# Moving the last token search behind five pairs of outputs, with MoE products over four PSUM banks, in a fused cross-covariance attention and mixture-of-depths kernel

## The chip, the cores and the metric

The kernel runs on one core of a Trainium2 chip. The metric is the time on the device in microseconds. Its engines are TensorE (PE in the profile; PEld is its weight load), VectorE (DVE), ScalarE (ACT), GpSimd (POOL) and SyncE (SP). SP only issues DMAs here; POOL issues DMAs too, the loads and the indirect ones.

## The reference

Two stages, over 4 batches of 6208 rows and 256 channels.

```python
qn = q / (norm(q, axis=1) + 1e-6);  kn = k / (norm(k, axis=1) + 1e-6)
a = softmax(kn.transpose(0, 2, 1) @ qn / tau)          # 256 x 256 per batch
x = v @ a                                              # 6208 x 256 per batch
scores = x @ w_gate                                    # one per row
for each batch: top = the 128 rows of the largest scores
    ye = relu(x[top] @ w1) @ w2                        # 256 -> 1024 -> 256
    out[top] = x[top] + sigmoid(scores[top]) * ye      # all other rows: out = x
```

Attention runs over channels, so all rows of q and k have to be read before the first row of the output can be computed. The 128 rows with the largest scores are known only when all scores of the batch are.

## The kernel before, in words

**Tiling.** A batch is cut into six chunks of 1024 rows (128 partitions of 8 rows) and a remainder of 64 rows. All loads of q, k and v are issued by POOL (`emit_load`, L166) and cast to bf16 on the way. The outputs of a chunk are collected in a tile `stage` of 1 MB and stored by one DMA of SP's queue (`emit_store`, L534).

**The main part.** For each batch a first pass accumulates the product of q and k (`s_ps`, L291) and the squares (`g_ps`, L293, L295) in PSUM. The softmax (`softmax_stages`) follows in small steps. The second pass transposes v (L403), evicts it (L410, L412), multiplies by the softmax matrix to give the output rows (`o_ps`, L477) and by the gate weights to give the scores (`sc_ps`, L431). An output pair is four matmuls (two rows of each partition) in one PSUM bank, evicted by one copy (L483 on VectorE or L485 on ScalarE). The order of all this is a written list, `plan` (L125 to L148). Batch 0 and 1 have their second pass inside the first pass of the following batch. Of batch 2 (`E`) most outputs, and of batch 3 (`L`) all of them, are left for the end; two late groups of batch 1 (`H`) get their MoE rows added by matmuls in `late_pair`.

**The search.** `select_stages` (L548) is a generator that finds the 128 rows with the largest scores: the scores are scaled to a range in which the threshold lies (`u`, L577), then seven rounds count the rows over seven thresholds (L585 or L587 compare, L591 counts on VectorE, a matmul at L598 sums over the partitions, L601 picks the interval). Then come the row numbers (L608 to L637) and an indirect DMA that gathers the rows of v (L641). `mlp_stages` (L649) is the MoE of one batch in steps: two transposes (L654), the attention product (L660), two transposes (L669), the gate (L674 to L679), the first product and Relu (L687, L690), the second product (L695), the update (L704) and an indirect DMA that scatters the rows into the output (L710). The scatter of a batch has to wait for the stores of that batch.

**The tail.** When all scores of batch 3 are there, the code from L838 on runs: two steps of the last search (its scores and maximum, then the scaling and the first comparison), the deferred stores, and then a loop of 40 output pairs: 15 of batch 2, then 25 of batch 3. After each pair `between` (L450) may take one more step of the last search, or, when that is at its end, one step of the MoE of batch 2:

```python
            due = pairs[0] in (2, 4, 6) or pairs[0] > 6 and pairs[0] % 5 in (0, 3)
            if due and not advance(side):
                advance_all(side2)
```

So the step that begins with the matmul of the first count (L598) is put into TensorE's order behind the second pair. All engines take their instructions in order. While the search runs, ScalarE evicts every pair; after it VectorE and ScalarE take turns (L482). In this loop `out_psum` (L438) hands out four banks in turn: one of `s_ps`, one of `g_ps` (both free by then) and the two of `ps_o`. Before the loop it hands out the two of `ps_o` alone. After the loop the store of the late chunk of batch 1 is issued, then 24 matmuls on constants (`keep_warm`, L415), the MoE of batch 3, and its scatter as the last transfer.

Of the kernel before, what the change touches and what calls it, by code (L numbers as in the profile page):

```python
# [9 lines left out]
F32 = mybir.dt.float32  # L10
# [4 lines left out]
ALU = mybir.AluOpType  # L15
AX = mybir.AxisListType

P = 128
# [1 line left out]
CHUNK = RPP * P  # L20
NTHR = 7
NSTEP = 7
NEG = -3.0e38


@with_exitstack
def kernel(
# [12 lines left out]
    nc = tc.nc  # L40

    B, N, C = q.shape
# [8 lines left out]
    REM = N - NFULL * CHUNK  # L51
    assert 0 < REM <= P
    NCOL = NFULL * RPP + 1
# [20 lines left out]
    moe = ctx.enter_context(tc.tile_pool(name="moe", bufs=1))  # L74
# [5 lines left out]
    ps_o = ctx.enter_context(tc.tile_pool(name="ps_o", bufs=2, space=PS))  # L80
# [69 lines left out]
    for op in plan:  # L150
        if op[0] in ("p1", "T"):
            u = ("qk", op[1], op[2]) if op[0] == "p1" else ("v", op[1], op[2][0])
# [102 lines left out]
    for i in range(NSTEP):  # L255
        w = 1.0 / (NTHR + 1) ** (i + 1)
        nc.vector.tensor_scalar(out=shares[:, i, :], in0=iota_row[:, 1:NTHR + 1], scalar1=w,
                                scalar2=None, op0=ALU.mult)
# [7 lines left out]
                            scalar2=None, op0=ALU.mult)  # L266
# [148 lines left out]
    def keep_warm(n):  # L415

        bank = ps_o.tile([P, 2, C], F32, name="o_ps")
        for _ in range(n):
            nc.tensor.matmul(bank[:, 0, 0:P], lhsT=ident_b, rhs=ones_b, start=True, stop=True)
# [18 lines left out]
    def out_psum():  # L438

        if now[0] <= B:  # L440
            return ps_o.tile([P, 2, C], F32, name="o_ps")
        turn[0] += 1
        if turn[0] % 4 == 1:
            return ps_s.tile([P, 2, C], F32, name="s_ps")
        if turn[0] % 4 == 3:
            return ps_g.tile([P, 4, P], F32, name="g_ps").rearrange("p a c -> p (a c)").rearrange(
                "p (a c) -> p a c", a=2)
        return ps_o.tile([P, 2, C], F32, name="o_ps")

    def between():  # L450

        if now[0] > B:
            pairs[0] += 1
            due = pairs[0] in (2, 4, 6) or pairs[0] > 6 and pairs[0] % 5 in (0, 3)
            if due and not advance(side):
                advance_all(side2)

    pairs = [0]
# [89 lines left out]
    def select_stages(b):  # L548

        sc_ps = sc_tiles[b]  # L550
        sc = moe.tile([P, NCOL], F32, name="sc")
        nc.vector.memset(sc[:, NCOL - 1:NCOL], NEG)
        u = moe.tile([P, NCOL], F32, name="u0")
        nc.vector.memset(u[:, NCOL - 1:NCOL], -1.0)  # L554
        nc.vector.tensor_reduce(out=sc[:, 0:NCOL - 1], in_=sc_ps[:, 0:NCOL - 1, :], axis=AX.X, op=ALU.add)
        nc.vector.tensor_reduce(out=sc[:REM, NCOL - 1:NCOL], in_=sc_ps[:REM, NCOL - 1:NCOL, :],
                                axis=AX.X, op=ALU.add)
# [8 lines left out]
        lo = moe.tile([P, 1], F32, name="lo")  # L566
        tops = moe.tile([P, 8], F32, name="tops")
        rng = moe.tile([P, 1], F32, name="rng")
        nc.vector.tensor_reduce(out=lo, in_=mps[:, 0:P], axis=AX.X, op=ALU.min)
        nc.vector.max(out=tops, in_=mps[:, 0:P])  # L570
        nc.vector.tensor_scalar(out=rng, in0=tops[:, 2:3], scalar1=lo, scalar2=1e-30, op0=ALU.subtract,
                                op1=ALU.max)
        nc.vector.reciprocal(rng, rng)


        for rows, cols in ((slice(0, P), slice(0, NCOL - 1)), (slice(0, REM), slice(NCOL - 1, NCOL))):
            nc.vector.tensor_scalar(out=u[rows, cols], in0=sc[rows, cols], scalar1=lo[rows], scalar2=rng[rows],  # L577
                                    op0=ALU.subtract, op1=ALU.mult)
        delta = None
        for i in range(NSTEP):  # L580
            cmp = moe.tile([P, NTHR, NCOL], BF16, name="cmp", bufs=2)
# [4 lines left out]
            else:  # L586
                nc.vector.scalar_tensor_tensor(out=cmp, in0=wide, scalar=delta, in1=thr,  # L587
                                               op0=ALU.subtract, op1=ALU.is_ge)
# [3 lines left out]
            if i > 0:  # L592
                nxt = moe.tile([P, NCOL], F32, name="u", bufs=2)
                nc.vector.tensor_scalar(out=nxt, in0=u, scalar1=delta, scalar2=None, op0=ALU.subtract)
                u = nxt
# [11 lines left out]
        with nc.allow_low_precision(reason="counts of at most 49 are whole in bf16"):  # L607
            nc.vector.scalar_tensor_tensor(out=msk, in0=u, scalar=delta, in1=zeros, op0=ALU.subtract,  # L608
                                           op1=ALU.is_ge, accum_out=own)
        nc.vector.tensor_tensor_scan(out=rhs[:, 0:NCOL], data0=ones_col, data1=msk, initial=0.0,  # L610
                                     op0=ALU.mult, op1=ALU.add)
# [10 lines left out]
                                       op1=ALU.mult)  # L622
# [8 lines left out]
                                       op0=ALU.is_le, op1=ALU.mult, accum_out=toff)  # L631
# [6 lines left out]
                                op0=ALU.max, op1=ALU.add)  # L638
# [10 lines left out]
    def mlp_stages(b):  # L649
        vg, idx, _ = gathered[b]  # L650
        a_sb, _ = a_tiles[b]
        tp = ps_vt.tile([P, 2, 4, P], BF16, name="vt_ps")
        for cc in range(2):
            nc.tensor.transpose(tp[:, cc, 0, :], in_=vg[:, cc * P:(cc + 1) * P], identity=ident_b)  # L654
        vgt = moe.tile([P, 2, P], BF16, name="vgt", bufs=2)
        nc.vector.tensor_copy(vgt, tp[:, :, 0, :])
        yield
        mps = ps_m.tile([P, 512], F32, name="m_ps")
        for cc in range(2):
            nc.tensor.matmul(mps[:, 0:C], lhsT=vgt[:, cc, :], rhs=a_sb[:, cc, :], start=cc == 0,  # L660
                             stop=cc == 1)
        xe = moe.tile([P, D], F32, name="xe", bufs=2)
        xe_b = moe.tile([P, D], BF16, name="xe_b", bufs=2)
        nc.vector.tensor_copy(xe_b, mps[:, 0:D])
        nc.vector.tensor_copy(xe, mps[:, 0:D])
        yield
        tp = ps_vt.tile([P, 2, 4, P], BF16, name="vt_ps")
        for dc in range(2):
            nc.tensor.transpose(tp[:, dc, 0, :], in_=xe_b[:, dc * P:(dc + 1) * P], identity=ident_b)  # L669
        xet = moe.tile([P, 2, P], BF16, name="xet", bufs=2)  # L670
        nc.vector.tensor_copy(xet, tp[:, :, 0, :])
        scj = moe.tile([P, D], BF16, name="scj")
        ssc = moe.tile([P, 1], F32, name="ssc")
        nc.vector.tensor_tensor_reduce(out=scj, in0=xe, in1=wg_bcast, scale=1.0, scalar=0.0, op0=ALU.mult,  # L674
                                       op1=ALU.add, accum_out=ssc)
        gate = moe.tile([P, 1], F32, name="gate", bufs=2)
        nc.scalar.activation(gate, ssc, AF.Exp, scale=-1.0)
        nc.vector.tensor_scalar_add(gate, gate, 1.0)
        nc.vector.reciprocal(gate, gate)  # L679
        yield  # L680
        h_sb = moe.tile([P, NFC, P], BF16, name="h_sb", bufs=2)
        for hf in range(NFC // 4):
            h_ps = ps_o.tile([P, 2, C], F32, name="o_ps").rearrange("p a c -> p (a c)")
            for f4 in range(4):
                fc = hf * 4 + f4
                for dc in range(2):
                    nc.tensor.matmul(h_ps[:, f4 * P:(f4 + 1) * P], lhsT=w1_sb[:, dc, fc * P:(fc + 1) * P],  # L687
                                     rhs=xet[:, dc, :], start=f4 == 0 and dc == 0,
                                     stop=f4 == 3 and dc == 1)
            nc.scalar.activation(h_sb[:, hf * 4:(hf + 1) * 4, :].rearrange("p f t -> p (f t)"), h_ps,  # L690
                                 AF.Relu)
        yield
        y_ps = ps_o.tile([P, 2, C], F32, name="o_ps")
        for fc in range(NFC):
            nc.tensor.matmul(y_ps[:, 0, :], lhsT=h_sb[:, fc, :], rhs=w2_sb[:, fc, :], start=fc == 0,  # L695
                             stop=fc == NFC - 1)
        upd = moe.tile([P, D], F32, name="upd", bufs=2)
        if b == H:
            gy = moe.tile([P, D], F32, name="gy")
            nc.vector.tensor_scalar(out=gy, in0=y_ps[:, 0, :], scalar1=gate, scalar2=None, op0=ALU.mult)  # L700
            nc.vector.tensor_tensor(out=upd, in0=gy, in1=xe, op=ALU.add)
            yield from late_parts(gy)
        else:
            nc.vector.scalar_tensor_tensor(out=upd, in0=y_ps[:, 0, :], scalar=gate, in1=xe, op0=ALU.mult,  # L704
                                           op1=ALU.add)
        yield
        yield
        while held[b] or (b >= E - 1 and deferred):
            yield
        ins = nc.gpsimd.indirect_dma_start(out=out_flat[0:(b + 1) * N, :],  # L710
                                           out_offset=bass.IndirectOffsetOnAxis(ap=idx[:, 0:1], axis=0),
                                           in_=upd, in_offset=None)
        scatters.append((b, ins))
        for o, sto in stores:
            if o != b:
                tc.declare_no_dep(ins.ins, sto.ins, reason="rows of different batches")
# [4 lines left out]
    def advance(lst):  # L721
        while lst:
            try:
                next(lst[0])
                return True
            except StopIteration:
                lst.pop(0)
        return False

    def advance_all(lst):  # L730
        for gen in list(lst):
            try:
                next(gen)
            except StopIteration:
                lst.remove(gen)
# [69 lines left out]
    for op in plan:  # L805
# [30 lines left out]
        else:  # L836
            side.append(select_stages(b))
    b = B - 1  # L838
    side.append(select_stages(b))
    advance(side)  # L840
    advance(side)
    flush_deferred()
    while side2:
        advance(side2)
    while waiting:
        side2.append(mlp_stages(waiting.pop(0)))
# [50 lines left out]
```

## Time and profile before

| | |
|---|---|
| median of 6 runs | 267.54 us (267.41 to 270.08) |
| profiled execution, its own time | 270.11 us |
| its span, first to last instruction | 268.4 us |
| busy share of the span: PE, PEld, DVE, ACT, POOL | 75%, 66%, 46%, 30%, 21% |
| moved by DMA | 66.97 MB, mean 250 GB/s |
| chain that ended last, by engine | PE 40%, DMA 32%, DVE 15% |

The profile is of one execution; its times are counted from the first instruction, and 1.7 us of the execution's time lie outside its span. A matmul is shown with a modelled end, so the distance from start to start is the better measure of what it takes. Times to landing are those from the issue of a DMA to its semaphore. "Granted clock" is the share of full speed at which TensorE was allowed to run. The DMA share is the mean busy share of the core's 16 DMA engines; packets are counted where they start, so that a short stretch can show more than 1.

### The profile page before, as it was taken

The page shows a single profiled execution, that of the slowest core. Times are in us where ns is not written, and L with a number is a line of the kernel's source. Part 1 is how long each engine was busy: PE and PEld are TensorE (multiplying, and loading weights), DVE is VectorE, ACT ScalarE, POOL GpSimd, SP SyncE. Part 2 cuts the span into 40 slices and gives each one's busy share as a digit, 9 for nine tenths or more (in the row PEclk, how much of TensorE's full clock was granted, in tenths as well). Part 3 has the DMA queues.
Part 4 walks back from the last instruction along what each step waited for, and adds up shares of the span by engine and source line. Part 5 has one row for each costly group of instructions (what it writes and reads, how often), then busy time and mean ns, then how long its engine had stood idle before and what let it go on. Part 6 is the DMA issues. An engine that isn't in the chain of part 4 may idle for free.

```text
span 268.4 us, 6081 instructions
## 1 busy us (share of the span) xinstructions
PE 201.0 (75%) x2576; PEld 177.8 (66%) x2576; DVE 124.0 (46%) x475; ACT 80.4 (30%) x143; POOL 56.0 (21%) x104
## 2 busy tenths in 40 slices
PE   0196868899935767899926978799999896888810
PEld 0185857789924656789815967698899894577600
DVE  0200003524305376614405886665785847876600
ACT  3101100177710000167600200434011873775310
POOL 7113123211110023312110326310441003010110
PEclk9997999999988799999967799999999998999985
DMA  6999999999999999999999999999999989999950
GB/s 215 231 229 231 210 212 214 215 215 297 313 320 314 281 212 214 212 215 289 326 254 214 211 222 212 212 214 212 190 168 215 214 310 383 397 368 372 420 230 0
DMA packets 17642, 66.97 MB, mean 250 GB/s; under 512 B 2000, under 2 KB 4688, under 8 KB 14544
## 3 DMA queue, kind: packets, MB, share of 16 engines
q0 software_dynamic: 12384, 38.93, 73.1%
q1 hardware_dynamic: 5232, 27.66, 26.0%
q8 instruction: 20, 0.33, 0.5%
q14 instruction: 6, 0.05, 0.0%
HBM read 79.04 MB, written 25.95 MB: 391 GB/s over the span
## 4 chain that ended last, share of the span: by engine, by line
PE 40%; DMA 32%; DVE 15%; issue 7%; ACT 1%; POOL 1%; POOLq 1%; DVEq 0%; SPq 0%
DMA k_ch<-in_k_dram 27%; PE s_ps L291 9%; PE o_ps L477 7%; PE g_ps L295 5%; PE g_ps L293 5%; PE vt_ps L403 4%; DMA q_ch<-in_q_dram 3%; DMA out_dram<-stage 3%; DVE cnt L591 2%; PE sc_ps L431 2%; DVE cmp L587 2%; DVE junk L310 2%; PE s_ps L477 1%; PE o_ps L687 1%; PE m_ps L342 1%
## 5 line engine op out<-in xcount | busy, mean ns | idle before, releaser
L291 PE MATMUL s_ps<-q_ch,k_ch 128*128 128x256 bf16 x384 | 96.4, 291 | 35.0 <-DMA k_ch<-in_k_dram 34.4
L293 PE MATMUL g_ps<-q_ch 128*128 128x128 bf16 x384 | 88.5, 230 | 1.1 <-DVE nsq L310 1.0
L295 PE MATMUL g_ps<-k_ch 128*128 128x128 bf16 x384 | 88.5, 230 | 0.0
L291 PEld LDWEIGHTS <-k_ch 128*128 128x128 bf16 x384 | 39.9, 104 | 40.6 <-DMA k_ch<-in_k_dram 37.5
L477 PE MATMUL o_ps<-a_sb,vt_sb 128*128 128x256 bf16 x298 | 44.6, 274 | 1.4 <-ACT vt_sb L410 1.3
L295 PEld LDWEIGHTS <-k_ch 128*128 128x128 bf16 x384 | 40.0, 104 | 8.5 <-issue 1.7
L293 PEld LDWEIGHTS <-q_ch 128*128 128x128 bf16 x384 | 39.9, 104 | 1.0 <-issue 0.6
L485 ACT COPY stage<-o_ps 128x512 f32<-128x512 f32 x64 | 36.0, 589 | 14.6 <-PE o_ps L477 14.3
L477 PEld LDWEIGHTS <-vt_sb 128*128 128x128 bf16 (+1 forms) x376 | 30.1, 99 | 9.2 <-issue 4.7
L412 DVE COPY vt_sb<-vt_ps 128x1024 bf16<-128x1024 bf16 (+1 forms) x33 | 20.8, 634 | 28.6 <-PE vt_ps L403 28.5
L174 POOL DMA_DIRECT2D q_ch<-in_q_dram x23 | 12.8, 559 | 63.5 <-PE g_ps L295 30.7
L431 PEld LDWEIGHTS <-vt_sb 128*128 128x128 bf16 (+1 forms) x376 | 23.8, 96 | 2.5 <-DVE u L554 0.2
L403 PE MATMUL vt_ps<-ident_b,v_ch 128*128 128x128 bf16 x336 | 24.6, 218 | 0.8 <-ACT vt_sb L410 0.7
L431 PE MATMUL sc_ps<-aw_sb,vt_sb 128*128 128x2 bf16 (+1 forms) x376 | 24.1, 164 | 0.0
L306 ACT COPY s_sb<-s_ps 128x512 f32<-128x512 f32 x4 | 2.3, 586 | 70.7 <-PE s_ps L291 40.6
L403 PEld LDWEIGHTS <-v_ch 128*128 128x128 bf16 x384 | 22.5, 97 | 1.4 <-issue 1.0
L310 DVE CUSTOM_DVE_ANT_0 junk<-g_ps,ident_f 128x128 f32<-128x128 f32 x16 | 4.7, 291 | 38.8 <-PE g_ps L295 38.4
L174 POOL DMA_DIRECT2D k_ch<-in_k_dram x23 | 12.6, 546 | 24.3 <-PE o_ps L477 7.0
L174 POOL DMA_DIRECT2D v_ch<-in_v_dram x24 | 12.9, 548 | 17.9 <-DMA k_ch<-in_k_dram 9.7
L591 DVE TENSOR_REDUCE cnt<-cmp 128x7 bf16<-128x343 bf16 x28 | 14.4, 513 | 1.0
L587 DVE SCALAR_TENSOR_TENSOR cmp<-u,delta,shares 128x343 bf16<-128x343 f32 x24 | 13.9, 579 | 0.9
L410 ACT COPY vt_sb<-vt_ps 128x1024 bf16<-128x1024 bf16 x11 | 10.6, 1012 | 10.9 <-PE vt_ps L403 10.9
(152 smaller groups left out, 218.4 us busy)
## 6 DMA issues: line engine op xcount, KB each, us to landing
out_dram<-stage SPq DMA_DIRECT2D x24, 1024.0 KB, 6.7
v_ch<-in_v_dram POOLq DMA_DIRECT2D x24, 512.0 KB, 14.8
q_ch<-in_q_dram POOLq DMA_DIRECT2D x23, 512.0 KB, 15.3
k_ch<-in_k_dram POOLq DMA_DIRECT2D x23, 512.0 KB, 22.2
stage<-in_moe_w_dram SPq DMA_DIRECT2D x2, 1024.0 KB, 24.4
q_ch<-in_q_dram POOLq DMA_DIRECT2D x2, 256.0 KB, 6.1
k_ch<-in_k_dram POOLq DMA_DIRECT2D x2, 256.0 KB
out_dram<-stage_rem SPq DMA_DIRECT2D x4, 64.0 KB, 13.4
```

The lines of the kernel that those rows point to most:

```text
L174: ins = nc.gpsimd.dma_start(out=t, in_=view(src, b, ci))
L291: nc.tensor.matmul(s_ps[:, cc, :], lhsT=ks[:, sl], rhs=qs, start=first and cc == 0, stop=last and cc == 1)
L293: nc.tensor.matmul(g_ps[:, cc, :], lhsT=qs[:, sl], rhs=qs[:, sl], start=first and cc == 0, stop=False)
L295: nc.tensor.matmul(g_ps[:, 2 + cc, :], lhsT=ks[:, sl], rhs=ks[:, sl], start=False, stop=last and cc == 1)
L403: nc.tensor.transpose(vt_ps[:, cc, j, :parts], in_=vt[:parts, s0 + j, cc * P:(cc + 1) * P], identity=ident_b[:parts, :parts])
L410: nc.scalar.copy(vt_sb[:, :, :n, :parts], vt_ps[:, :, :n, :parts])
L412: nc.vector.tensor_copy(vt_sb[:, :, :n, :parts], vt_ps[:, :, :n, :parts])
L431: nc.tensor.matmul(sc_ps[:parts, col, :], lhsT=vt_sb[:, cc, j, :parts], rhs=aw_sb[:, cc, :], start=cc == 0 and col in (0, NCOL - 1), stop= ...
L477: nc.tensor.matmul(o_ps[:parts, pj, :], lhsT=vt_sb[:, cc, j, :parts], rhs=a_sb[:, cc, :], start=pj == 0 and cc == 0, stop=pj == m - 1 and ...
L485: nc.scalar.copy(st[:parts, s0 + pair * 2:s0 + pair * 2 + m, :], o_ps[:parts, :m, :])
L587: nc.vector.scalar_tensor_tensor(out=cmp, in0=wide, scalar=delta, in1=thr, op0=ALU.subtract, op1=ALU.is_ge)
L591: nc.vector.tensor_reduce(out=cnt, in_=cmp, axis=AX.X, op=ALU.add)
```

## The change

Four edits. `between` takes no step before the fifth pair, so that the first count is behind five pairs and each later step two or three pairs further back; from pair 8 on the rule for the due pairs is the same, but each of them takes an earlier step than it did. In `mlp_stages` the banks of the two halves of the first product and of the second product come from `out_psum`, which in the tail's loop and after it means four banks in turn. The scaled scores `u` are computed by one operation over all 49 columns instead of two (48 whole columns, and 64 partitions of the last); the filler of the unused rows and the smallest range are changed so that this stays finite, and the memset of `u` goes. `keep_warm(8)` is put between the first and the second step of the last search.

```diff
-NEG = -3.0e38
+NEG = -1.0e20
...
-            due = pairs[0] in (2, 4, 6) or pairs[0] > 6 and pairs[0] % 5 in (0, 3)
+            due = pairs[0] >= 5 and pairs[0] % 5 in (0, 3)
...
-        u = moe.tile([P, NCOL], F32, name="u0")
-        nc.vector.memset(u[:, NCOL - 1:NCOL], -1.0)
...
-        nc.vector.tensor_scalar(out=rng, in0=tops[:, 2:3], scalar1=lo, scalar2=1e-30, op0=ALU.subtract,
+        nc.vector.tensor_scalar(out=rng, in0=tops[:, 2:3], scalar1=lo, scalar2=1e-18, op0=ALU.subtract,
                                 op1=ALU.max)
...
-        for rows, cols in ((slice(0, P), slice(0, NCOL - 1)), (slice(0, REM), slice(NCOL - 1, NCOL))):
-            nc.vector.tensor_scalar(out=u[rows, cols], in0=sc[rows, cols], scalar1=lo[rows], scalar2=rng[rows],
-                                    op0=ALU.subtract, op1=ALU.mult)
+        u = moe.tile([P, NCOL], F32, name="u", bufs=2)
+        nc.vector.tensor_scalar(out=u, in0=sc, scalar1=lo, scalar2=rng, op0=ALU.subtract, op1=ALU.mult)
...
-            h_ps = ps_o.tile([P, 2, C], F32, name="o_ps").rearrange("p a c -> p (a c)")
+            h_ps = out_psum().rearrange("p a c -> p (a c)")
...
-        y_ps = ps_o.tile([P, 2, C], F32, name="o_ps")
+        y_ps = out_psum()
...
     side.append(select_stages(b))
     advance(side)
+    keep_warm(8)
     advance(side)
     flush_deferred()
```

## The prediction

> **What bounds the kernel now.** I read the chain of waits first, from its end backwards, because only what stands on it can move the time. Columns: start, length, what.
>
> ```profile
> 246.52 0.87 PE o_ps L695 x8
> ...
> 250.48 0.70 DVE stage L483
> 251.24 6.74 DMA out_dram<-stage
> ...
> 258.67 1.20 POOLq L892
> ```
>
> The kernel ends with the scatter of the last batch (it starts at 258.89 and everything after it takes 9.5 us to the span's end at 268.4). It waits for the last batch's last store, issued at 251.24 and landed at 257.98. The scatter's other input, the MoE update, was done at 256.84 (L704: 256.36 + 0.48), so the MoE chain of the last batch has 2.0 us of slack. The store itself is late because of its evictions, which follow the output pairs on TensorE. So next the timeline of TensorE from 222 us on, where the last search begins.
>
> ```profile
> 222.74 0.46 PE L562 MATMUL m_ps<-ident_f,mx 128*128 128x128 f32 x2 [0.74 <-DVE mx L559]
> ...
> 225.85 0.17 PE L598 MATMUL m_ps<-cnt,ones_b 128*128 128x7 bf16 x1 [1.78 <-DVE cnt L591]
> 225.87 1.02 PE L477 MATMUL g_ps<-a_sb,vt_sb 128*128 128x256 bf16 x4
> ...
> 230.82 0.60 PE L477 MATMUL s_ps<-a_sb,vt_sb 128*128 128x256 bf16 x4
> ...
> 244.60 0.61 PE L687 MATMUL o_ps<-xet,w_sb 128*128 128x128 bf16 x8 [0.94 <-ACT h_sb L690]
> ```
>
> TensorE computes two pairs, stands 1.78 us for the first count, and then runs pairs 3 to 6 at half clock (the granted clock of 225.5 to 229 is 0.51; a pair takes 0.85 to 0.88 from start to start instead of 0.44). Further stalls of 0.5 to 0.6 us follow at the counts, and one of 0.94 in the MoE of batch 2. That is some 5 us of lost TensorE time. But the pairs only feed the stores, so I asked how busy the DMA engines are meanwhile. Columns: stretch, length, busy time of PE, PEld, DVE, ACT, POOL, clock, DMA share, GB/s.
>
> ```profile
> 230.00:246.00 16.00, 13.18 (x125) 10.46 (x123) 11.97 (x44) 11.51 (x24) 0.97 (x1) 1.00 0.94 366
> 246.00:258.00 12.00, 8.79 (x95) 7.05 (x93) 6.37 (x15) 3.95 (x8) 0.98 (x1) 1.00 1.01 420
> ```
>
> From 246 to 258 the engines are full with stores; from 230 to 246 they are nearly full. The queue that issues the stores does wait for evictions:
>
> ```profile
> SPq L536 <- ACT stage L485: 15.7, 8, 5.5
> SPq L536 <- DVE stage L483: 10.5, 5, 3.6
> ```
>
> Hence the tail has two limits close together: pairs that come too late, and store bandwidth. The pairs' gain counts only up to what the DMA engines had free.
>
> **The order of the pairs.** The tail has 40 pairs. The search needs ten steps: seven counts, then own/scan, the one-hot, and the gather. Before, the steps stand behind pairs 2, 4, 6, 8, 10, 13, 15, 18, 20, 23; after, behind 5, 8, 10, 13, 15, 18, 20, 23, 25, 28. The MoE of batch 2 starts with the tenth step and takes the next due pairs: 23, 25, 28, 30, 33 before, 28, 30, 33, 35, 38 after.
>
> I timed the new order from rows. A pair takes TensorE 0.44 (223.03 to 223.47). An eviction starts 0.48 after the last one on ScalarE (223.67 to 224.15). A count follows the last by 1.59 where it waits for VectorE alone (229.20, 230.79, 232.38, 233.97, 235.56). Five pairs from 223.03 end at 225.2. The first count's input is there at 225.79 before, and about 225.55 after (below). So TensorE waits 0.3 us instead of 1.78. Then counts come at 227.2, 228.8, 230.4, 232.0, 233.5, 235.1; the last three steps take as long as before (235.56 to the gather's 239.53), so the gather comes at 239.1. Between counts lie 2.5 pairs, 1.1 us of TensorE and 1.2 us of ScalarE in 1.59, so the pairs keep up and the search isn't delayed. At 239.1 there are 28 pairs done instead of 23.
>
> What remains is 12 pairs at 0.44 (5.3 us), the MoE of batch 2 on TensorE (16 products at 0.056, eight in 0.87, the transposes and two products some 0.44: 2.2 us), and a stall of about 0.7, because one pair's bank is evicted by VectorE behind the gate operations (L678). So the pairs end at 247.3, against 250.3 before, and the last store is issued at 248.2 instead of 251.24. The stores of four-pair chunks ahead of it move from 229.91, 232.55, 235.24, 238.72, 240.90, 242.86, 246.87, 249.49 to about 227.0, 229.4, 231.7, 235.2, 237.7, 239.6, 242.5, 245.5: each some 3 to 4 us earlier.
>
> **What the stores make of it.** A 1 MB store takes 2.5 us of full engines (1.05 MB at 420 GB/s), and the new issue times are closer together than that or as close. So from 228 us on the queue never runs dry, and the last store lands when the sum is moved. What is won is the engines' free time between 230 and 246: by the share 16 x (1.01 - 0.94) = 1.1 us; by the bytes 16 x (1 - 366/420) = 2.1 us, of which about 0.5 us is the gather's small packets and stays. A third count goes by issue times: where a store came after the one ahead was drained (at 229.91, 232.55, 235.24, 238.72; 1.4 us from issue to first packet) the gaps come to 0.9, 0.25, 0.2 and 0.6, 1.9 us together. I take 1.5 us, between 1.1 and 2.1. The stall removed on TensorE is thus worth half of its 3.0 us; the rest turns into queueing, and the last store's 6.74 us to landing grow to about 8.
>
> The Trainium skill, page "DMA: Bandwidth & Descriptors", section "Where 436 GB/s comes from", says that transfers between HBM and SBUF are bound on the HBM side at about 358 GB/s for a core, not by the fabric's 435. The row of 246 to 258 shows 420, so that bound does not hold here. By it, 230 to 246 with 366 GB/s would already be full and this estimate would be a gain of nothing.
>
> **The MoE over four banks.** Before, both halves of h and y share two banks with every second pair, and the second half waits 0.94 us for a VectorE eviction. After, in the tail they take the next of four banks. This concerns batches 2 and 3 only; for the two earlier ones the function returns the same pool. In batch 2 the 0.94 goes; the pairs behind may wait up to 0.3 us more for a Relu. Both lie under the full store queue, so nothing is added to the sum. In batch 3 the 16 products run unbroken before (253.93, x16 in 1.05), so nothing is to be won.
>
> **Eight warming matmuls.** 24 of them before L654 take 250.35 to 251.69, 0.056 each: eight take 0.45 us. They start at 222.0 and end in the 0.74 us that L562 waits for the maximum on VectorE, so they cost nothing. At half clock they would take 0.9 and delay the search by 0.2 us, which the update's slack covers. The gain side is in the pairs above: with the warming and five pairs TensorE works 80% of 222.1 to 225.5, and I expect pairs 3 to 6 at 0.44.
>
> **Scaled scores in one operation.** L577's two instructions (0.48 us) become one of 128x49, which costs 0.24 (L594: same operation and shape). One memset of 0.06 goes, which lies in the wait for the scores. So every search is 0.24 us shorter. The first three lie under loads at a DMA share of 0.99: nothing. In the last it brings the first count forward (used above). The other constant changes no instruction.
>
> **The sum.** The profiled execution took 270.11 us with its span of 268.4; the median of the runs is 267.54, so it was 2.6 above. Scatter from 258.89 to 257.4, the span 266.9, the profiled time 268.6. On the median: 267.54 - 1.5 = 266.0.
>
> **Rivals.**
> (1) The stores are at their limit already: the 0.94 is uneven engines, not a dry queue. For it: single microseconds in that stretch show shares of 0.7 next to 1.1. Against it: the waits of the store queue, and a store issued at 246.87 that landed in 4.5 us, the shortest of all, so nothing was queued ahead of it. Then only 0 to 0.5 us is won: 267.0 to 267.5. Chance 0.10.
> (2) The whole 3 us arrive: the last store lands 6.74 after its issue as before. Time 267.54 - 3.0 = 264.5. It would need the engines to move a further 0.6 MB in the same time, for which no stretch of the tail shows a rate. Landing times are uneven, though (4.5 to 11.4 us for the stores of the tail). Everything over 2.1 counts here: 0.16.
> (3) Slower: the last batch's gather sinks in the deeper store backlog and the MoE chain becomes the end. Gathers so far:
>
> ```profile
> DMA to landing us min/median/max: 6.4/13.5/20.6
> ```
>
> From transposes to update the chain takes 5.15 us (251.69 to 256.84). With the gather issued at 239.1 it decides from a landing of 14.6 us on (258.89 - 5.15 - 239.1). At 20.6 the scatter would start at 264.9: +6.0, 273.5. Against it: the 20.6 stood behind loads on the gather's own software queue, of which none is left in the tail; the last gather, beside stores on the other queue, took 6.4. Chance 0.10.
>
> **How the numbers follow.** The forecast (1.1 to 2.1 us won) has 0.64. A measurement of this kernel can tell about 0.5%, 1.34 us, from no change; of the forecast's span some 0.44 lies beyond it, 0.20 within. Faster: 0.44 + 0.16 = 0.60; same: 0.20 + 0.10 = 0.30; slower: 0.10. The range takes in the forecast (265.4 to 266.4), rival 1 up to 267.5 and most of rival 2, down to 264.7.
>
> **What would show it.** Right: the 1.78 us ahead of the first count falls under 0.5; the clock of 225.5 to 229 is near 1; the last store of batch 3 is issued near 248 and lands after about 8 us; the DMA share of 230 to 246 rises to about 1.0 and 410 GB/s; the scatter starts near 257.4 with the update done by 254. Wrong: a scatter that waits for the update or the gather; counts more than 1.6 us apart, TensorE or ScalarE being late; a share still at 0.94 with the stores issued 3 us earlier (rival 1); or a last store landing in under 7 us (rival 2).

## The result, and the profile after

The changed kernel takes 265.88 us (median of 20 runs), the one before 267.71 us (median of 46). The ratio is 0.9923, with a 95% interval from 0.9904 to 0.9943: 2.06 us faster, between 1.5 and 2.6. The ratio is taken over all runs; the two medians lie 1.83 us apart. The prediction was 266.0.

One thing is needed to compare the two profiles: in the profiled execution of before the load that releases the first deferred store landed 2.6 us later than in this one (216.09 and 213.48), and some runs of either kernel are longer than the rest by about as much. So I compare times of the tail from its first deferred store on, which is issued at 216.11 before and at 213.50 after; 2.61 is added to a time of after where the two stand side by side.

The chain that ended last, at its end (start, length, what):

```profile
244.78 0.70 DVE stage L483
245.53 7.84 DMA out_dram<-stage
...
254.06 1.19 POOLq L890
```

The chain has the same form as before. The last store of batch 3 is issued at 245.53, which is 248.14 on the scale of before (251.24 there, 248.2 foretold). It took 7.84 us to land instead of 6.74. From the first deferred store to this landing it is 253.37 - 213.50 = 39.87 us; before it was 257.98 - 216.11 = 41.87. From this landing to the end of the span it is 10.42 us in both, so these 2.00 us are the whole change.

The timeline of TensorE:

```profile
220.15 0.46 PE L560 MATMUL m_ps<-ident_f,mx 128*128 128x128 f32 x2 [0.18 <-DVE mx L557]
...
223.13 0.17 PE L595 MATMUL m_ps<-cnt,ones_b 128*128 128x7 bf16 x1 [0.34 <-DVE cnt L588]
223.16 0.60 PE L477 MATMUL o_ps<-a_sb,vt_sb 128*128 128x256 bf16 x4
...
240.48 0.61 PE L684 MATMUL s_ps<-xet,w_sb 128*128 128x128 bf16 x8
241.52 0.60 PE L477 MATMUL o_ps<-a_sb,vt_sb 128*128 128x256 bf16 x4 [0.44 <-ACT h_sb L687]
```

The wait for the first count is 0.34 us (1.78 before), the warming matmuls cut the wait for the maximum from 0.74 to 0.18, and the pairs run at full clock (1.00 from 220 to 227). The second half of h no longer waits; a wait of 0.44 stands behind it, at the next pair.

The busy time of the engines (PE, PEld, DVE, ACT, POOL), the clock, the DMA share and GB/s, for about the stretches shown of before:

```profile
227.00:243.00 16.00, 14.11 (x135) 11.43 (x133) 12.13 (x44) 12.66 (x26) 0.96 (x1) 1.00 1.02 401
243.00:251.00 8.00, 6.03 (x70) 4.58 (x68) 4.25 (x12) 2.10 (x5) 0.98 (x1) 1.00 1.01 422
```

By the share the first stretch has become as full as the second: 1.02 where before 0.94 stood. By the bytes it moves 401 GB/s instead of 366, and the second 422.

### The profile page after: what moved, and what is told of

It is laid out like the page before. It is cut to its first block, busy times and chain, and to the rows that moved or that the text cites. A ratio compares the mean times of both kernels' runs of the same rounds, so it can differ in the third digit from the quotient of the medians.

```text
span 263.8 us, 6087 instructions
## 1 busy us (share of the span) xinstructions
PE 200.5 (76%) x2584; PEld 176.6 (67%) x2584; DVE 121.2 (46%) x464; ACT 81.6 (31%) x146; POOL 55.5 (21%) x104
## 4 chain that ended last, share of the span: by engine, by line
DMA 59%; PE 15%; issue 11%; DVE 9%; POOL 1%; ACT 1%; POOLq 1%; DVEq 0%; SPq 0%
DMA k_ch<-in_k_dram 30%; DMA v_ch<-in_v_dram 17%; DMA q_ch<-in_q_dram 9%; PE o_ps L477 5%; DMA out_dram<-stage 3%; PE s_ps L291 2%; DVE cnt L588 2%; PE vt_ps L403 2%; DVE cmp L584 2%; PE g_ps L295 1%; PE g_ps L293 1%; PE sc_ps L431 1%; DVE stage L483 1%; PE g_ps L477 1%; PE m_ps L595 1%
## 5 line engine op out<-in xcount | busy, mean ns | idle before, releaser
L477 PE MATMUL o_ps<-a_sb,vt_sb 128*128 128x256 bf16 x298 | 43.9, 271 | 1.9 <-ACT vt_sb L410 1.3
L485 ACT COPY stage<-o_ps 128x512 f32<-128x512 f32 x68 | 38.3, 590 | 15.6 <-PE o_ps L477 15.6
L477 PEld LDWEIGHTS <-vt_sb 128*128 128x128 bf16 (+1 forms) x376 | 29.4, 97 | 8.1 <-issue 4.4
L431 PEld LDWEIGHTS <-vt_sb 128*128 128x128 bf16 (+1 forms) x376 | 23.8, 96 | 2.5 <-DVE sc L552 0.2
## 6 DMA issues: line engine op xcount, KB each, us to landing
stage<-in_moe_w_dram SPq DMA_DIRECT2D x2, 1024.0 KB, 23.4
```

Of the source, the lines that this page charges most:

```text
L431: nc.tensor.matmul(sc_ps[:parts, col, :], lhsT=vt_sb[:, cc, j, :parts], rhs=aw_sb[:, cc, :], start=cc == 0 and col in (0, NCOL - 1), stop= ...
L477: nc.tensor.matmul(o_ps[:parts, pj, :], lhsT=vt_sb[:, cc, j, :parts], rhs=a_sb[:, cc, :], start=pj == 0 and cc == 0, stop=pj == m - 1 and ...
L485: nc.scalar.copy(st[:parts, s0 + pair * 2:s0 + pair * 2 + m, :], o_ps[:parts, :m, :])
```

## The experiments

Two questions were open: which of the four edits does it, and whether the end follows the DMA engines or the pairs. Differences are between medians of the same set of runs; the ratios are over all runs of a set, and the two can differ by some tenths of a microsecond.

**The parts alone.** Each is one edit of the change on the kernel before.

```diff
# order_only
-            due = pairs[0] in (2, 4, 6) or pairs[0] > 6 and pairs[0] % 5 in (0, 3)
+            due = pairs[0] >= 5 and pairs[0] % 5 in (0, 3)
# banks_only
-            h_ps = ps_o.tile([P, 2, C], F32, name="o_ps").rearrange("p a c -> p (a c)")
+            h_ps = out_psum().rearrange("p a c -> p (a c)")
...
-        y_ps = ps_o.tile([P, 2, C], F32, name="o_ps")
+        y_ps = out_psum()
# warm_only
     advance(side)
+    keep_warm(8)
     advance(side)
```

> The kernel before with the new due pairs alone (no warming matmuls, no four banks, two operations for the scaled scores). Theory A (the tail ends when the stores are moved; what counts is how long the DMA engines stood dry between the first deferred store and the last): the stores of batch 2 and 3 are issued some 3 us earlier, the dry stretches go, and nearly all of the change's gain comes from here: 1.5 to 2.0 us faster than before. Rival B (the end follows the last pair on TensorE, one for one): the last pair ends about 2 us earlier without the bank edit, so about 2 us as well, but the last store's time to landing stays at 6 to 7 us; under A it grows to about 8. Rival C (the half clock of TensorE is the cause, and the warming matmuls the cure): pairs 3 to 6 still run at half clock and under 0.8 us is won.

Measured: 265.94 us against 267.74, 1.80 faster, ratio 0.9940 (0.9927 to 0.9952). The order alone brings nearly everything. Its profile settles something more:

```profile
247.16 6.45 DMA out_dram<-stage
...
220.00:224.00 4.00, 3.92 (x20) 2.98 (x21) 2.38 (x8) 1.77 (x4) 1.32 (x2) 0.57 1.01 391
227.00:243.00 16.00, 13.23 (x125) 10.62 (x125) 12.41 (x47) 12.41 (x26) 0.96 (x1) 1.00 1.00 400
```

Without the warming the clock fell to half (0.57 in the row from 220 to 224) and the first pairs took 0.85 us each, as before. Yet the DMA share from 227 to 243 is full and the time is that of the whole change. Its last store is issued at 247.16, 1.7 us later than in the changed kernel, and lands only 0.3 us later, both counted from the first deferred store (253.60 - 213.44 = 40.16). So half clock is not what cost the time.

One sign missed. Theory A wanted the last store's time to landing to grow to about 8 us, rival B to stay at 6 to 7, and it is 6.45. Counted from the first deferred store, this last store is issued 1.4 us earlier than before and lands 1.7 us earlier, so this run taken alone does not tell the two theories apart. Beside the changed kernel it does, where an issue 1.7 us earlier brings only 0.3 us.

> The kernel before with the MoE products over four banks alone. Theory A: the 0.94 us stall in the MoE of batch 2 goes, and as the store issued next (246.87 in the profile before) landed in 4.5 us with nothing queued ahead of it, its delay was on the path: 0.4 to 0.9 us faster than before. The prediction had put this edit at nothing, hidden under the full store queue; if it holds in the old order too, under 0.2 us is won.

Measured: 267.61 us against 267.74, ratio 1.0001 (0.9980 to 1.0021): nothing that can be told. The stall of 0.94 is gone from its trace and the store behind it is issued 0.6 us earlier, but the last store still lands 42.2 us after the first deferred one. The expectation of 0.4 to 0.9 was wrong; the prediction's nothing was right.

> The kernel before with the eight warming matmuls alone. Theory A: the clock may stay full after the wait for the first count, but pairs 3 to 6 then stand longer at the counts, which come every 1.6 us whatever TensorE does: 0 to 0.4 us faster. Rival C (the half clock is the cause): over 1 us faster.

Measured: 267.41 us against 267.74, ratio 0.9973 (0.9946 to 1.0000): a few tenths at the edge of the noise, and nothing in its profile, where the last scatter starts 42.80 us after the first deferred store (42.78 before). The warming did not keep the clock in this execution: it is 0.51 from 223.3 to 226.7. TensorE still stands 1.82 us for the first count.

> The changed kernel with the old due pairs: warming matmuls, four banks and scaled scores in one operation remain. The first two were worth 0.1 to 0.3 us by themselves; if the order is nearly all of the change, 0.1 to 0.5 us faster than before. If the parts only work together (the warming keeps the clock for the pairs, the banks keep them running), over 0.8 us faster.

```diff
# on the changed kernel
-            due = pairs[0] >= 5 and pairs[0] % 5 in (0, 3)
+            due = pairs[0] in (2, 4, 6) or pairs[0] > 6 and pairs[0] % 5 in (0, 3)
```

Measured: 267.27 us against 267.88 before, ratio 0.9992 (0.9966 to 1.0017). Three edits of four together give 0.6 us by the medians and 0.2 by the ratio, not clear of the noise, so the gain is in the main the order's and not an interplay.

**Are the DMA engines the limit?** The next edit leaves the work of all engines but SP as it is. The store of the late chunk of batch 1, which is issued last though its data are ready before the loop, goes among the deferred stores. The scatter of batch 1, which waits for that batch's stores, moves with it: it starts 11.5 us after the first deferred store instead of 7.7 (11.5 instead of 8.3 in the changed kernel, on which the same edit follows below).

```diff
+    deferred.insert(2, (H, NFULL - 1))
     flush_deferred()
...
-    emit_store(H, NFULL - 1)
```

> The kernel before, all engines but SP unchanged: the store of the late chunk of batch 1, whose data are ready before the tail's loop, is issued with the deferred stores instead of at the very end. Theory A: this megabyte fills the dry stretches that late pairs leave, and the last store of batch 3 no longer shares the engines with it: 1.0 to 1.8 us faster than before with TensorE's work and stalls as before. Rival B (the end follows the pairs): the last pair ends when it did and the last store is issued when it was, so 0 to 0.3 us.

Measured: 268.81 us against 267.74, 1.07 slower, ratio 1.0051 (1.0024 to 1.0079). Both theories failed here in sign. The chain's end shows why:

```profile
248.81 7.54 DMA out_dram<-stage
256.35 0.02 issue
```

The last store is issued at the same moment as before, counted from the first deferred one (35.4 against 35.1 us), but takes 7.5 us to land. The stores land in the order of their issue: in order_only, where both landings were recorded, the late chunk's store landed 2.43 us behind the last one of batch 3 (256.03 after 253.60). In its old place it is therefore behind the store that the scatter waits for. Ahead of it, it should cost its 2.5 us, less the dry time it fills. So the theory had to be mended: the end is the moment when all bytes queued ahead of the last awaited store are moved. This predicts that the same edit on the changed kernel, where no dry time is left, costs the full 2.5 us.

> The changed kernel once more, beside the three others of this set, which are compared with it: 1.8 to 2.1 us faster than before.

Measured: 265.83 us against 267.74, 1.91 faster, ratio 0.9925 (0.9898 to 0.9953).

> The changed kernel with the late chunk's store of batch 1 issued among the deferred stores instead of last. The same edit on the kernel before cost 1.1 us, and not the gain that theory A had foretold, because the store in its old place stands behind the one that the scatter waits for. Theory A mended (the end is the moment when all bytes queued ahead of the last awaited store are moved): the megabyte costs its 2.5 us of full engines, less the dry time it fills. The dry time was 2.5 - 1.1 = 1.4 us before; it should be near 0 after, so 2.2 to 2.6 us slower than the changed kernel. Rival B (the end follows the last pair on TensorE): 0 to 0.3 us slower, as no pair moves. Rival D (a new floor after the change is the update of the last batch, not the stores): under 1 us slower.

Measured: 268.04 us, 2.21 slower than the changed kernel beside it; the ratio to before is 0.9998 (0.9974 to 1.0022).

```profile
245.57 10.14 DMA out_dram<-stage
255.71 0.02 issue
```

The issue has not moved (245.53 in the changed kernel), and the landing is 2.3 us later with all the time in the queue. The same megabyte costs 1.07 us before and 2.21 after: 1.1 us of dry time were there to be filled before and are not there after. By the ratios the two costs are 1.4 and 2.0 us, and their intervals overlap. The profiles are clearer: from the first deferred store to the landing of the last awaited one it is 42.94 us instead of 41.87 before and 42.23 instead of 39.87 after, 1.1 and 2.4 us more. By the medians and the profiles the megabyte costs 2.2 to 2.4 us ahead of the awaited store, out of the 2.5 that it takes, so it can have cost at most some 0.3 us in its place behind it (0.5 by the ratios). The pairs as the limit (rival B) and the update as the new floor (rival D) are both out.

**Is a late pair free after the change?** 24 matmuls on constants, 1.3 us of TensorE, behind the 26th pair of each kernel.

```diff
             pairs[0] += 1
+            if pairs[0] == 26:
+                keep_warm(24)
```

> The kernel before with 24 matmuls on constants (1.3 us of TensorE) put behind the 26th pair, in front of the pairs of the store that landed with nothing queued ahead of it. Theory A mended: that store comes 1.1 to 1.3 us later and so does the end: 0.8 to 1.3 us slower than before. Rival B: 1.3 us.

Measured: 268.61 us against 267.74, 0.87 slower, ratio 1.0032 (1.0005 to 1.0059). Both theories allow this, as both expected about the same here. The profile does not show the cost. Counted from the issue of the gather, the last store is issued 1.3 us later than before (13.0 us against 11.7) but lands at the same time (18.4 us in both); in this execution the first stores went out earlier against the pairs, with the gather 25.3 us behind the first deferred store instead of 23.4. It shows another limit:

```profile
252.72 5.37 DMA out_dram<-stage
POOL out_dram L712 <- DVE upd L706: 17.4, 2, 9.0
```

The store lands at 258.09, the update of the last batch ends at 258.33, and the second line says that the scatter waits for the update. The 24 matmuls stand ahead of the MoE of batch 3 too, and have used up the 1.1 us that its update was ahead of the landing (256.84 and 257.98 before). So that a late pair costs time before rests on the times of the runs, and whether through the store or the update is not shown.

> The changed kernel with the same 24 matmuls behind the 26th pair. Theory A mended: the stores behind them stand 2 to 3 us in a full queue and the update has 2.3 us of slack, so 0 to 0.3 us slower than the changed kernel. Rival B (the end follows the pairs): 1.3 us slower, as before. Rival D (the update of the last batch is the floor): 1.0 to 1.3 us slower.

Measured: 266.06 us, 0.23 over the changed kernel beside it; the ratios to before, 0.9921 (0.9891 to 0.9951) and 0.9925, don't differ.

```profile
246.96 6.41 DMA out_dram<-stage
253.37 0.02 issue
```

Its last store is issued 1.4 us later than in the changed kernel (245.53) and lands at the same 253.37. A delay that costs 0.87 us before costs nothing that can be told after, where the queue swallows it (the two costs are not far enough apart to be told by the intervals alone). This is the cover named in the prediction, measured on the changed kernel.

**The rest of the gain.** The pair of store_early runs accounts for some 1.1 us of 2.0. A second count comes from the whole way from the first deferred store to the landing of the last awaited one, before and after:

```profile
216.11:257.98 41.87, 33.35 (x397) 27.19 (x395) 27.05 (x92) 23.02 (x44) 3.98 (x4) 0.96 0.97 386
213.50:253.37 39.87, 32.38 (x401) 26.70 (x401) 24.94 (x87) 23.54 (x45) 3.96 (x4) 0.99 1.01 402
```

The mean rate rose from 386 to 402 GB/s. At 402 GB/s the bytes of before would take 40.2 us, so 1.7 of the 2.0 us are time in which the engines were dry or slow. The other 0.3 us are 0.13 MB less that is moved up to the landing. The gain becomes visible late, between two landings: the store of L's fifth chunk lands 4.2 us behind the fourth before (255.52 and 251.34), 2.2 us after (250.64 and 248.40). The scatter of batch 2 lies in that stretch. It was left out, with its rows not written, in both kernels:

```diff
+        if b == E:
+            return
         ins = nc.gpsimd.indirect_dma_start(out=out_flat[0:(b + 1) * N, :],
```

> The kernel before without the scatter of batch 2 (its MoE rows are not written). Open is 0.9 us of the 2.0 that the change won from the first deferred store to the landing of the last: by bytes moved its stores are 1.1 us ahead. Between the landings of the last but two and the last but one store lie 4.2 us before and 2.2 after, and in that stretch the scatter of batch 2 lands (0.13 MB, 0.3 us of full engines). Theory E (the scatter runs on few of the 16 engines, a store ends with its slowest engine, and with a short queue this is not made good): 0.8 to 1.5 us faster than before. Theory A alone: 0.2 to 0.4 us.

Measured: 267.25 us against 267.88, 0.63 faster, ratio 0.9980 (0.9960 to 1.0001).

> The changed kernel without the scatter of batch 2. Theory E (a full queue evens out the engines): 0.2 to 0.4 us faster than the changed kernel, less than the same edit brings before. Theory A alone: 0.2 to 0.4 us in both.

Measured: 265.54 us, ratio to before 0.9918 (0.9887 to 0.9948). The changed kernel, in other sets, has 0.9923 and 0.9925, so this is 0.1 to 0.2 us under it. The order of the two results is that of theory E, but the first is below what it asked for, neither is clear of the noise, and without the scatter the two landings before still lie 3.5 us apart (252.39 and 248.85). So the scatter explains a few tenths at best. Counted from the first deferred store, the fourth landing after the change is only 0.3 us ahead of before, the fifth 2.3 us. Why nearly all of the gain shows between the two stays open.

**Dry time taken away elsewhere.** The changed kernel still has a dry stretch where the loads end and the first stores begin. There the first deferred store was made to wait for one load earlier.

```diff
-                st.ins, load_inst[units[-3]].ins.name,
+                st.ins, load_inst[units[-4]].ins.name,
```

> The changed kernel with the first deferred store waiting for one load earlier, so that stores start some 2.5 us sooner and the engines' dry time between the last loads and the first stores goes (shares of 0.79, 0.62 and 0.94 in the three microseconds around the first store: 0.65 us). Theory A mended: the stores end 0.3 to 0.7 us earlier, if the last loads, which now share the engines, delay the last scores by no more than the 3 us of slack that the update has: 0.3 to 0.7 us faster than the changed kernel. Otherwise the update of the last batch becomes the end: 0 to 1 us slower.

Measured: 267.43 us against 267.88 before, ratio 0.9993 (0.9971 to 1.0014), so 1.6 us slower than the changed kernel's 265.83 in another set, and 1.8 by the ratios. The worse branch of the expectation came, beyond its 1 us and by another way than it said. Four stretches of this kernel:

```profile
212.00:214.00 2.00, 1.95 (x22) 1.55 (x21) 0.00 (x0) 1.42 (x3) 0.00 (x0) 1.00 1.09 313
...
222.00:224.00 2.00, 1.81 (x34) 1.59 (x32) 0.98 (x6) 0.00 (x0) 1.13 (x2) 1.00 0.60 250
224.00:226.00 2.00, 1.98 (x19) 1.62 (x17) 1.83 (x7) 1.73 (x4) 0.89 (x1) 1.00 0.63 168
226.00:228.00 2.00, 1.63 (x15) 1.31 (x15) 1.65 (x6) 1.97 (x5) 0.00 (x0) 1.00 0.96 397
```

The gap at the first store is closed (1.09 where the changed kernel has 0.71). But the last loads share the engines with the early stores and land 2.9 us later (218.87 for the remainder of v, 216.01 in the changed kernel). The last scores and all pairs shift by 3.2 us, and between 222 and 226 the queue runs dry for some 1.5 us (shares of 0.60 and 0.63). The scatter still waits for the store, which lands at 255.01, not for the update, which ends at 254.23. It is the same law from the other side: dry time was moved, not removed, and made longer.

## Why the prediction was right, and which term was small

**The order of the pairs.** Right in its times. On the scale of before, the eight stores ahead of the last were foretold at 227.0, 229.4, 231.7, 235.2, 237.7, 239.6, 242.5, 245.5 and came at 227.0, 229.1, 231.8, 235.5, 238.0, 240.1, 242.4, 245.5. The gather was issued at 239.3 (239.1 foretold); counts stayed 1.59 us apart (224.73, 226.32, 227.91, 229.50). The steps behind the first count stand four or five pairs further back than before (the second behind pair 8 instead of 4, the last behind 28 instead of 23), and not two or three as the section on the change says.

**Half of what TensorE wins turns into queueing.** Right in kind; it was a third. The last store came 3.1 us earlier and landed 2.0 us earlier; its time to landing rose to 7.84 (about 8 foretold). delay_after shows the queue as a cover, and the two store_early runs price it. The reason given was not sound: the foretold issues are not all 2.5 us apart or closer (235.2 - 231.7 = 3.5, and 2.9, 3.0 and 2.7 at the end). The queue stayed full because stores were waiting in it: those of the changed kernel from 222 us on whose landings were recorded took 7.2 to 8.6 us from issue to landing, against 4.5 for the quickest before.

**The size.** 1.5 us was foretold, and 2.06 measured by the ratio, 1.83 by the medians and 2.00 in the profiles. The term that was too small is the free time of the engines between 230 and 246. I had three counts, 1.1 by the share, 2.1 by the bytes less 0.5 for the gather, and 1.9 by the issue times, and took a value in the lower half. The share rose to 1.02 and not to the 1.01 of the later stretch, which makes 1.3 us; over the whole way the rate accounts for 1.7. The 0.5 us for the gather was an estimate that no run tested. The count by issue times came closest, but in part by luck: no run shows its 1.4 us from issue to first packet. In the profile before, the first deferred store is issued at 216.11; up to 216.90 the DMA engines move at most 16 GB/s, and in the next 0.2 us 635. That is 0.8 us. That 266.0 came so near to 265.88 has some luck too: the gain was larger than foretold, and the median of before is 267.71 in the larger set, where the sum had started from 267.54.

**The edits put at nothing.** The banks alone 1.0001, the warming alone 0.9973, and both with the scaled scores 0.9992: nothing or a few tenths. In batch 2 the wait behind the Relu came, 0.44 us where up to 0.3 was foretold, and lies under the full queue. What I said of the clock, that the warming and five pairs keep it full, held in the changed kernel (1.00 from 220 to 223.5), but as order_only shows it has hardly a price behind a full queue (0.3 us in the landing).

**The scaled scores.** One operation of 128x49 was put at 0.24 us by the subtraction of L594. It took 0.35:

```profile
221.63 0.35 DVE L575 TENSOR_SCALAR u<-sc,lo,rng 128x49 f32<-128x49 f32 x1
222.01 0.52 DVE L582 TENSOR_TENSOR cmp<-u,shares 128x343 bf16<-128x343 f32 x1
```

From its start to the next operation it is 0.38 where the two took 0.51, so a search is 0.13 us shorter and not 0.24. It has two scalars and two operations, L594 one, and I had matched the shape alone; which of the two costs the 0.11 us was not tested.

**The rivals.** (1) Stores at their limit already: refuted, the share rose from 0.94 to 1.02. By the figure of 358 GB/s in the Trainium skill, page "DMA: Bandwidth & Descriptors", section "Where 436 GB/s comes from", the stretch could not have gone from 366 to 401. (2) All 3 us arrive: refuted, the landing time grew. (3) The gather sinks in the backlog: it did take longer, 8.5 us instead of 6.4, and the last batch's update was done at 251.09, 3.2 us ahead of the scatter and 2.3 ahead of the store's landing. The limit of 14.6 us was set too high, as it is counted to the old start of the scatter. The scatter started 0.9 us after the landing that it waited for, so the update has to be done at about the landing itself. Counted so, the slack before was 1.1 us and not 2.0, and with the landing foretold 1.5 us earlier the gather would have decided from some 12 us on (257.98 - 1.5 - 5.15 - 239.1). At 8.5 us it was far from that too.

## What to carry to other kernels

When a chain ends with a store, ask two things before pricing a faster producer: how long the DMA engines stood dry or slow since the queue was last full, for that is about all that was won here (1.7 of 2.0 us), and which bytes stand ahead of the store that somebody waits for. Behind the awaited store a megabyte cost at most some 0.3 us here; ahead of it, it cost 2.2 us with a full queue and 1.1 us where it filled a gap. And an edit that fills a gap at one place has to be checked for the transfers that it delays: starting the stores earlier delayed the loads, and the gap came back larger downstream.

## What was not expected of the hardware

The clock fell to half in stretches of 3.4 us or twice that. Each of the six profiled kernels without the warming has such a stretch that begins between 220 and 226 us. Of the six with the warming and the new order none has one behind the warming, up to the end of the last batch's products. With the warming and the old order the two profiles differ: warm_only had 0.51 from 223.3 to 226.7 and after_old_order 1.00 in the same microseconds, though TensorE stood for the first count in both, 1.82 and 1.65 us. What decides this was not settled. And stores of the same size on one queue landed 2.2 to 4.2 us apart at DMA shares of 1.0 in both cases, so a share of 1.0 doesn't say that a given store is moving at the full rate.
